# One PSUM ring of three double banks for scores, values and gate tiles, with score bursts of three chunks

## The chip, the cores and the metric

One core of a Trainium2 chip. The metric is the time of one execution in microseconds (us), measured on the device; all times below are us unless marked ns. Fast executions of one kernel spread over 1 to 5 us, so each comparison says how many runs it rests on. A time ratio is the mean over the fast runs of one kernel divided by the mean over the fast runs of the kernel before in the same rounds on the same chip, so it is not quite the ratio of the medians quoted. The comparisons were made on four occasions, each with its own runs of the kernel before; only ratios, and periods within one trace, are compared across them.

The granted clock (the share of full speed that TensorE got, averaged over an execution) differs between executions of one kernel and matters for such small differences. In executions at 0.993 to 0.996 the time is longer than in those at 0.998 or more: 375.3 (9 runs) against 373.5 (11) in e1, 376.1 (11) against 374.2 (8) in e3, 376.9 (7) against 375.1 (5) in e6. The two profiles in that state (e1, e6) show the clock halved for 3.4 us of the passage from batch 0 to batch 1, at 57.6 and 57.1, and not in the loop. Ratios of kernels with different shares of such executions have to be read with this in mind.

## The reference, cut to what matters

Causal attention over 8 batches and 8 heads, 576 queries of 64, with 16 extra "beacon" keys in front that every query sees, followed by a gated feed-forward layer on the 4608 tokens.

```python
scores = scale * np.matmul(q, k_all.transpose(0, 1, 3, 2))   # k_all: 16 beacons + 576 keys
scores = np.where(causal, -1e9, scores)
a = softmax(scores)                                          # written out in the reference
x = np.matmul(a, v_all)                                      # then to (4608, 512)
g = x @ w_gate                                               # 512 -> 1536
out = (gelu(g) * (x @ w_val)) @ w_out                        # 1536 -> 512
```

## The kernel before

The work is a loop over batches. In each, TensorE (PE) runs attention of batch b mixed with 48 output matmuls of batch b-1 (`o(n)` issues n of them), then 12 gate/value tiles. Heads go in four pairs. The causal scores of a pair are cut into four chunks, 0 to 3, of 512, 480, 464 and 208 columns; `scores(b, (m, c))` computes chunk c of pair m for both heads into one double PSUM bank, from which ScalarE takes the exponential. `av(b, m)` multiplies with the values into an `x_ps` tile and has VectorE normalize it into `y_sb`. GpSimd (POOL) zeroes the masked triangle of each diagonal tile, for b > 0, and also issues all casting loads, in order.

PSUM has eight banks: two double tiles for scores and gate tiles, one double tile for values, two single ones. The parts that matter (cuts marked `...`):

```python
psum_s = tile_pool("psum_s", bufs=2, PSUM)   # scores, gate/value: 2 x 2 banks
psum_t = tile_pool("psum_t", bufs=1, PSUM)   # 1 bank
psum_x = tile_pool("psum_x", bufs=1, PSUM)   # values: 2 banks
psum_o = tile_pool("psum_o", bufs=1, PSUM)   # 1 bank
...
warm(8, psum_x, "x")        # 8 matmuls of 512 columns, before the first data
...
if b:
    o(4);  scores(b, (0, 0)); scores(b, (0, 2))
    ...                            # batch 1 only: one transpose of its inputs
    ahead(2); o(7);  scores(b, (0, 1)); scores(b, (0, 3), (1, 3))
    ahead(2); o(7);  scores(b, (1, 0)); scores(b, (1, 2))
    av(b, 0); turn_dma(b, 0)
    o(4);  scores(b, (1, 1)); scores(b, (2, 0))
    ahead(2); o(7);  scores(b, (2, 1)); scores(b, (2, 2))
    av(b, 1); turn_dma(b, 1)
    o(4);  scores(b, (2, 3), (3, 3)); scores(b, (3, 0))
    o(6);  av(b, 2)
    scores(b, (3, 1)); scores(b, (3, 2))
    o(4);  turn(b, 2); put(b, 2)      # transposes of the result on PE
    o(5);  av(b, 3)
```

`ahead(n)` issues n loads for batch 2; it does something in batch 1 only, after an `ahead(5)` in front of the whole computation's masks. After the attention part come `load_v(b+1)`, `load_qk(b+2)` (GpSimd) and `transpose_dma(b+1)` (transposing loads from SBUF to SBUF on the sync queue).

The softmax here doesn't subtract the row's maximum and nothing guards it: scores larger than these inputs give would overflow.

## Time and profile before

| | before |
|---|---|
| time, median (4 runs of the first comparison) | 375.18 |
| profiled span | 372.9 |
| PE busy | 365.0 (98%) |
| period of the loop (starts of the same matmul in successive batches) | 39.72 |
| third gate tile of batch 0 starts at | 28.09 |
| first gate matmul on the single bank (`g_ps`), batch 1, starts at | 87.96 |

The last two rows cut the span into start, passage from batch 0 to batch 1, and loop; the whole argument uses these three pieces. The profile lines themselves stand in the prediction. One caution in reading them: ends of matmuls are modelled, and too late (a matmul of 512 columns is listed as 0.38 long where the next starts after 0.216), so idle time of PE is listed too short, and waits under 0.15 are not listed at all. Starts are to be trusted: the difference between two starts minus the known streaming time is what PE lost.

### The profile page before, as it was taken

Reading aid. Unit: us, or ns where it says so; the run is one execution under the profiler, and the core shown is the slowest. Engines: PE = TensorE matmul, PEld = TensorE weight load, DVE = VectorE, ACT = ScalarE, POOL = GpSimd, SP = SyncE. Lnnn points to the kernel's source line nnn. Section 1 sums busy time; section 2 is a strip of 40 time slices with the busy share of each in tenths; the row PEclk is TensorE's granted clock in tenths of the full one; section 3 lists DMA queues with packets and bytes.
Section 4 is the critical chain, followed back from the end, with each engine's and each line's share of the span. In section 5 each row is a group of like instructions: output and inputs, shape, how many; then the busy total and the mean of one; then the engine's idle time right before and its main releaser. Section 6 shows DMA issues by size and latency. Waiting matters only on the chain.

```text
span 372.9 us, 7489 instructions
## 1 busy us (share of the span) xinstructions
PE 365.0 (98%) x3030; PEld 181.7 (49%) x3030; DVE 151.7 (41%) x253; ACT 188.4 (51%) x240; POOL 166.1 (45%) x293
## 2 busy tenths in 40 slices
PE   7999989999999999999999999999999999999996
PEld 3664535544554446444554455445544464444443
DVE  3354643543344425433444335333444244424332
ACT  4864267435753487338733774357534873332210
POOL 8965578860478145843495148625600330000000
PEclk9699999999999999999999999999999999999999
DMA  7999999999169913999299929991590030000103
GB/s 102 123 177 197 205 161 145 135 145 114 46 123 143 154 37 94 152 134 90 62 142 152 88 78 126 125 142 48 120 161 16 33 87 30 0 0 30 56 33 109
DMA packets 152050, 38.33 MB, mean 103 GB/s; under 512 B 136528, under 2 KB 147536, under 8 KB 152016
## 3 DMA queue, kind: packets, MB, share of 16 engines
q0 software_dynamic: 107184, 19.13, 69.9%
q1 hardware_dynamic: 44832, 18.73, 27.2%
q8 instruction: 24, 0.39, 0.5%
q14 instruction: 10, 0.08, 0.1%
HBM read 38.27 MB, written 9.44 MB: 128 GB/s over the span
## 4 chain that ended last, share of the span: by engine, by line
PE 95%; DVE 2%; DMA 1%; ACT 1%; issue 1%; POOL 0%; POOLq 0%
PE gv_ps L173 46%; PE o_ps L173 26%; PE s_ps L173 8%; PE x_ps L173 8%; PE v_ps L173 2%; PE g_ps L173 1%; PE y_ps L181 1%; DMA qk<-in_k_dram 1%; PE t_ps L181 1%; DVE qkT L199 1%; DVE qkT L215 0%; DVE hT_sb L424 0%; ACT ge_sb L176 0%; ACT expT L176 0%; POOL qk L113 0%
## 5 line engine op out<-in xcount | busy, mean ns | idle before, releaser
L176 ACT ACTIVATE ge_sb<-gv_ps 128x512 bf16<-128x512 f32 x101 | 59.4, 597 | 133.0 <-PE gv_ps L173 133.0
L176 ACT ACTIVATE expT<-s_ps 128x960 bf16<-128x960 f32 (+3 forms) x112 | 101.8, 960 | 28.2 <-PE s_ps L173 24.9
L424 DVE TENSOR_TENSOR hT_sb<-gv_ps,ge_sb 128x512 bf16<-128x512 f32 x101 | 69.2, 691 | 106.2 <-ACT ge_sb L176 106.2
L173 PE MATMUL gv_ps<-xT_sb,wg_sb 128*128 128x512 bf16 x404 | 108.1, 379 | 0.0
L173 PE MATMUL gv_ps<-xT_sb,wv_sb 128*128 128x512 bf16 x404 | 108.1, 379 | 0.0
L173 PE MATMUL o_ps<-wo_sb,hT_sb 128*128 128x512 bf16 (+2 forms) x444 | 105.9, 374 | 0.0
L289 POOL TENSOR_SCALAR_AFFINE_SELECT expT<-expT 128x256 bf16<-128x256 bf16 (+2 forms) x140 | 51.7, 386 | 102.1 <-ACT expT L176 94.6
L173 PEld LDWEIGHTS <-wv_sb 128*128 128x128 bf16 x432 | 42.2, 98 | 51.8 <-DVE qkT L204 1.4
L173 PEld LDWEIGHTS <-wg_sb 128*128 128x128 bf16 x432 | 41.2, 98 | 46.7
L173 PEld LDWEIGHTS <-hT_sb 128*128 128x128 bf16 x444 | 38.7, 98 | 46.4 <-issue 8.9
L443 DVE COPY o_sb<-o_ps 128x512 f32<-128x512 f32 (+2 forms) x37 | 25.0, 676 | 44.0 <-PE o_ps L173 43.9
L113 POOL DMA_DIRECT2D v_sb<-in_v_dram x45 | 36.6, 837 | 3.0 <-DMA wo_sb<-in_moe_w_out_dram 1.7
L173 PE MATMUL s_ps<-qkT 64*128 64x512 bf16 (+5 forms) x384 | 36.2, 289 | 1.2 <-ACT qkT L176 0.7
L173 PEld LDWEIGHTS <-expT 128*128 128x128 bf16 (+1 forms) x960 | 32.3, 97 | 8.1 <-POOL expT L289 2.3
L113 POOL DMA_DIRECT2D k_sb<-in_k_dram x30 | 25.2, 844 | 21.7 <-DMA q_sb<-in_q_dram 13.2
L173 PE MATMUL x_ps<-v_sb,expT 128*128 128x65 bf16 x930 | 33.9, 193 | 0.6 <-issue 0.6
L113 POOL DMA_DIRECT2D q_sb<-in_q_dram x30 | 25.3, 887 | 3.6 <-DMA wo_sb<-in_moe_w_out_dram 3.6
L349 DVE TENSOR_TENSOR y_sb<-x_ps,r_sb 128x640 bf16<-128x640 f32 x31 | 25.6, 824 | 1.1
L173 PEld LDWEIGHTS <-qkT 64*128 64x128 bf16 x384 | 14.0, 95 | 21.6 <-issue 17.9
L347 DVE RECIPROCAL r_sb<-x_ps 128x10 f32<-128x10 f32 x31 | 6.9, 221 | 40.4 <-PE x_ps L173 40.4
L382 DVE COPY xT_sb<-y_ps 128x576 bf16<-128x576 bf16 x15 | 6.9, 458 | 11.5 <-PE y_ps L181 11.5
L610 ACT ACT_TABLE_LOAD x7 | 9.0, 1283 | 0.1
(50 smaller groups left out, 126.1 us busy)
## 6 DMA issues: line engine op xcount, KB each, us to landing
out_dram<-o_sb SPq DMA_DIRECT2D x35, 256.0 KB, 2.2
q_sb<-in_q_dram POOLq DMA_DIRECT2D x24, 128.0 KB, 9.1
v_sb<-in_v_dram POOLq DMA_DIRECT2D x21, 128.0 KB, 6.5
k_sb<-in_k_dram POOLq DMA_DIRECT2D x18, 128.0 KB, 9.9
wg_sb<-in_moe_w_gate_dram POOLq DMA_DIRECT2D x6, 256.0 KB, 8.9
wv_sb<-in_moe_w_val_dram POOLq DMA_DIRECT2D x6, 256.0 KB, 9.0
wo_sb<-in_moe_w_out_dram POOLq DMA_DIRECT2D x3, 512.0 KB, 11.9
v_sb<-in_v_dram POOLq DMA_DIRECT2D x7, 112.0 KB, 4.2
```

The source lines that it names most:

```text
L113: keep(nc.gpsimd.dma_start(out=out_ap, in_=in_ap))
L173: keep(nc.tensor.matmul(out_ap, lhsT, rhs, start=start, stop=stop, **kw))
L176: keep(nc.scalar.activation(out_ap, in_ap, func, **kw))
L181: keep(nc.tensor.transpose(out_ap, in_ap, ident[0:n, 0:n]))
L199: nc.vector.tensor_copy(qkT[:, m, :, NB:SK].rearrange("p w (t r) -> p w t r", r=6), t_ps[:, 0:2, 0:S].rearrange("p w (r t) -> p w t r", r=6),)
L289: nc.gpsimd.affine_select(out=d, in_=d, pattern=[[0, 2], [1, n]], compare_op=ALU.is_ge, fill=0.0, base=NB if t == 0 else 0, channel_multip ...
L347: keep(nc.vector.reciprocal(r, x[:, :, :, D:DV]))
L349: nc.vector.tensor_tensor(out=y_sb[:, :, h0:h1, :].rearrange("p j b d -> p b j d"), in0=x[:, :, :, 0:D], in1=r.to_broadcast([P, h1 - h0, 5 ...
L382: keep(nc.vector.tensor_copy(out_ap, y_ps[:, 0:S]))
L424: nc.vector.tensor_tensor(out=h_of[ci][:, fi, :], in0=gv_of.pop((ci, fi))[1], in1=ge_sb, op=ALU.mult)
L443: keep(nc.vector.tensor_copy(o_sb[:, ti, c0:c1], o_ps))
L610: keep(nc.scalar.preload_act_table_set(SET_GELU))
```

## The change

Its intent: give the double banks of the value tile to the ring, so that it has three, write score chunks in five bursts (four of three tiles, one of two) instead of seven of two, and let batch 0 run its chunks two ahead of ScalarE. The warm-up changes too: 100 matmuls of 64 columns.

```diff
-    psum_s = ... bufs=2
+    psum_s = ... bufs=3
-    psum_x = ...
...
-    warm(8, psum_x, "x")
+    warm(100)                       # 64 columns each, from the ring
-    transpose_half(0, 0, 1); transpose_half(0, 0, 0, by_act=True)
+    transpose_both(0, 0)
     c((0, 0)); c((0, 2))
...                                  # batch 0: transposes and chunks further apart
-            x = pool.tile(..., tag=where)          # psum_x by default
+            x = psum_s.tile([P, 2, 512], ..., tag="s")
...
             o(4)
             scores(b, (0, 0)); scores(b, (0, 2))
-            o(7)
             scores(b, (0, 1))
+            o(5); ahead(2); o(5)
             scores(b, (0, 3), (1, 3))
-            ahead(2); o(7)
             scores(b, (1, 0)); scores(b, (1, 2))
+            ahead(2); o(6)
             av(b, 0); turn_dma(b, 0)
-            o(4)
+            o(2)
             scores(b, (1, 1)); scores(b, (2, 0))
-            ahead(2); o(7); scores(b, (2, 1))
             scores(b, (2, 2))
+            ahead(2); o(6)
             av(b, 1); turn_dma(b, 1)
-            o(4)
+            o(2)
+            scores(b, (2, 1))
             scores(b, (2, 3), (3, 3)); scores(b, (3, 0))
-            o(6); av(b, 2)
+            o(10)
             scores(b, (3, 1)); scores(b, (3, 2))
-            o(4)
+            av(b, 2); o(5)
             turn(b, 2); put(b, 2)
-            o(5)
+            o(3)
             av(b, 3)
```

Transposes of batch 1 on PE move: two stay between gate tiles of batch 0, two now follow the first burst of batch 1.

More of the change, by code (lines that the diff above doesn't have):

```diff
@@ L73 @@
     opool = ctx.enter_context(tc.tile_pool(name="opool", bufs=2))
-    psum_s = ctx.enter_context(tc.tile_pool(name="psum_s", bufs=2, space=bass.MemoryType.PSUM))
+    psum_s = ctx.enter_context(tc.tile_pool(name="psum_s", bufs=3, space=bass.MemoryType.PSUM))
     psum_t = ctx.enter_context(tc.tile_pool(name="psum_t", bufs=1, space=bass.MemoryType.PSUM))
-    psum_x = ctx.enter_context(tc.tile_pool(name="psum_x", bufs=1, space=bass.MemoryType.PSUM))
     psum_o = ctx.enter_context(tc.tile_pool(name="psum_o", bufs=1, space=bass.MemoryType.PSUM))
@@ L81 @@
     ident = eye[:, 64:192]
-    idle = const.tile([P, 512], BF16, name="idle", tag="idle")
+    idle = const.tile([P, P], BF16, name="idle", tag="idle")
     nc.vector.memset(idle, 0.0)
@@ L194, in transpose_pe @@
     def transpose_pe(b, m):
-        t_ps = psum_x.tile([P, 2, 1024], BF16, name="t_ps", tag="x")
+        t_ps = psum_s.tile([P, 2, 1024], BF16, name="t_ps", tag="s")
         for w in range(2):
@@ L215, in transpose_half, with beacon_part, transpose_both, warm @@
             keep(nc.vector.tensor_copy(out_ap, in_ap))
-        if w:
-            keep(nc.vector.tensor_copy(qkT[:, m, 1, 0:NB], t_ps[:, S:SK]))
-    def warm(n, pool, tag):
-        w_ps = pool.tile([P, D_MODEL], FP32, name="w_ps", tag=tag)
+        return t_ps
+    def beacon_part(m, t_ps):
+        keep(nc.vector.tensor_copy(qkT[:, m, 1, 0:NB], t_ps[:, S:SK]))
+    def transpose_both(b, m):
+        k_ps = transpose_half(b, m, 1)
+        transpose_half(b, m, 0, by_act=m == 0)
+        beacon_part(m, k_ps)
+    def warm(n):
+        w_ps = psum_s.tile([P, 2, 512], FP32, name="w_ps", tag="s")
         for j in range(n):
-            mm(w_ps, idle[:, 128 * (j % 4) : 128 * (j % 4) + 128], idle, True, True)
+            mm(w_ps[:, 0, 0:D], idle, idle[:, 0:D], True, True)
     def transpose_dma(b):
@@ L300, with attend @@
     x_of = {}
-    def attend(b, m, where="x", heads=(0, 1)):
+    def attend(b, m, where="s", heads=(0, 1)):
         i = b * NPAIR + m
@@ L330, in attend_tiles @@
         else:
-            pool = psum_s if where == "s" else psum_x
-            x = pool.tile([P, 2, 512], FP32, name="x_ps", tag=where)
+            x = psum_s.tile([P, 2, 512], FP32, name="x_ps", tag="s")
             x_ps = (x[:, 0, :], x[:, 1, :])
@@ L386, with gv_mms @@
     gv_of = {}
-    def gv_mms(ci, fi, *kks, where="s", last=False):
+    def gv_mms(ci, fi, *kks, split=False, last=False):
         if (ci, fi) not in gv_of:
-            if where == "tx":
+            if split:
                 gv_of[ci, fi] = (
                     psum_t.tile([P, CH], FP32, name="g_ps", tag="t"),
-                    psum_x.tile([P, CH], FP32, name="v_ps", tag="x"),
+                    psum_s.tile([P, 2, CH], FP32, name="v_ps", tag="s")[:, 0, :],
                 )
             else:
-                pool = psum_s if where == "s" else psum_x
-                gv_ps = pool.tile([P, 2, CH], FP32, name="gv_ps", tag=where)
+                gv_ps = psum_s.tile([P, 2, CH], FP32, name="gv_ps", tag="s")
                 gv_of[ci, fi] = (gv_ps[:, 0, :], gv_ps[:, 1, :])
@@ L412, in gv_mms @@
         part(0)
-        if where != "tx":
+        if not split:
             part(1)
@@ L418, in gv_mms @@
         act(ge_sb, gv_of[ci, fi][0], ACT.Gelu)
-        if where == "tx":
+        if split:
             part(1)
@@ L427, in gv_mms, with gate_val @@
         )
-    def gate_val(ci, fi, where="s"):
-        gv_mms(ci, fi, *range(K_CHUNKS), where=where, last=True)
+    def gate_val(ci, fi, split=False):
+        gv_mms(ci, fi, *range(K_CHUNKS), split=split, last=True)
     def out_mm(ci, ti, fi, o_ps, c0=0, c1=D_MODEL):
@@ L509, with av @@
     ahead(5)
-    def av(b, m, where="x"):
+    def av(b, m, where="s"):
         attend(b, m, where)
@@ L518 @@
     keep(nc.scalar.preload_act_table_set(SET_EXP))
-    warm(8, psum_x, "x")
+    warm(100)
     keep(nc.vector.tensor_copy(qk6[0][1], kb_sb))
-    transpose_half(0, 0, 1)
-    transpose_half(0, 0, 0, by_act=True)
+    transpose_both(0, 0)
     c((0, 0))
     c((0, 2))
-    transpose_half(0, 1, 1)
-    transpose_half(0, 1, 0)
+    transpose_both(0, 1)
     c((0, 1))
     c((1, 0))
-    transpose_half(0, 2, 1)
     c((1, 2))
-    transpose_half(0, 2, 0)
+    transpose_both(0, 2)
     c((0, 3), (1, 3))
     c((1, 1))
-    transpose_half(0, 3, 1)
     c((2, 0))
-    transpose_half(0, 3, 0)
+    transpose_both(0, 3)
     c((2, 2))
     c((2, 1))
-    attend(0, 0, "x", (0,))
+    av(0, 0)
     c((3, 0))
-    attend(0, 0, "x", (1,))
-    normalize(0, 0)
     c((3, 2))
-    attend(0, 1, "ot", (0,))
+    av(0, 1, "ot")
     c((2, 3), (3, 3))
-    attend(0, 1, "ot", (1,))
-    normalize(0, 1)
     c((3, 1))
@@ L553 @@
     put(0, 1, by_act=True)
-    av(0, 3, "s")
+    av(0, 3)
     gv_mms(0, 0, 0)
@@ L558 @@
     keep(nc.scalar.preload_act_table_set(SET_GELU))
-    gv_mms(0, 1, 0, where="x")
+    gv_mms(0, 1, 0)
     turn(0, 3, psum_o, "o")
@@ L576 @@
             scores(b, (0, 2))
+            scores(b, (0, 1))
+            if b == 1:
+                transpose_pe(1, 2)
+            o(5)
+            ahead(2)
             if b == 1:
                 transpose_pe(1, 3)
-            ahead(2)
-            o(7)
-            scores(b, (0, 1))
+            o(5)
             scores(b, (0, 3), (1, 3))
-            ahead(2)
-            o(7)
             scores(b, (1, 0))
             scores(b, (1, 2))
+            ahead(2)
+            o(6)
             av(b, 0)
             turn_dma(b, 0)
-            o(4)
+            o(2)
             scores(b, (1, 1))
             scores(b, (2, 0))
+            scores(b, (2, 2))
             ahead(2)
-            o(7)
-            scores(b, (2, 1))
-            scores(b, (2, 2))
+            o(6)
             av(b, 1)
             turn_dma(b, 1)
-            o(4)
+            o(2)
+            scores(b, (2, 1))
             scores(b, (2, 3), (3, 3))
             scores(b, (3, 0))
-            o(6)
-            av(b, 2)
+            o(10)
             scores(b, (3, 1))
             scores(b, (3, 2))
-            o(4)
+            av(b, 2)
+            o(5)
             turn(b, 2)
             put(b, 2)
-            o(5)
+            o(3)
             av(b, 3)
@@ L619 @@
             if fi >= 2:
-                gate_val(b, fi, "x" if b and fi == 2 else "tx" if fi == F_TILES - 1 and b < B - 1 else "s")
-            if b == 0 and 8 <= fi < 11:
+                gate_val(b, fi, fi == F_TILES - 1 and b < B - 1)
+            if b == 0 and fi in (8, 9):
                 transpose_pe(1, fi - 8)
```

## The prediction

> **What bounds the kernel now.** I read the page first: busy shares, clock row, chain.
>
> ```profile
> PE 365.0 (98%) x3030; PEld 181.7 (49%) x3030; DVE 151.7 (41%) x253; ACT 188.4 (51%) x240; POOL 166.1 (45%) x293
> ...
> PEclk9699999999999999999999999999999999999999
> ...
> PE 95%; DVE 2%; DMA 1%; ACT 1%; issue 1%; POOL 0%; POOLq 0%
> ```
>
> TensorE (PE) is busy 98% of the span and makes 95% of the chain that ended last. Only the second slice has a low clock. Busy matmuls are modelled, so I read real rates from starts. In the windows view one period of the attention/feed-forward loop, and the attention part of it alone, look so:
>
> ```profile
> 88.83:128.55 39.72, 39.72 (x324) 19.47 (x322) 16.07 (x27) 22.34 (x28) 20.99 (x37) 1.00 1.19 113
> 89.69:108.43 18.74, 18.74 (x222) 9.81 (x221) 7.05 (x12) 15.23 (x16) 8.28 (x22) 1.00 0.46 76
> ```
>
> No PE idle in either. The waits view for PE lists only small items, all from the start and the passage from batch 0 to batch 1; these matter here:
>
> ```profile
> PE v_ps L173 <- DVE qkT L204: 0.9, 1, 0.9
> PE s_ps L173 <- ACT qkT L176: 0.7, 1, 0.7
> PE x_ps L173 <- issue: 0.6, 1, 0.6
> ```
>
> So there is little to win except what PE itself spends without streaming columns. The timeline of the second attention stage shows what happens round a score burst:
>
> ```profile
> 96.40 1.03 PE L173 MATMUL o_ps<-wo_sb,hT_sb 128*128 128x512 bf16 x4
> ...
> 96.60 0.22 DVE L347 RECIPROCAL r_sb<-x_ps 128x10 f32<-128x10 f32 x1 [2.14 <-PE x_ps L173]
> 96.85 0.82 DVE L349 TENSOR_TENSOR y_sb<-x_ps,r_sb 128x640 bf16<-128x640 f32 x1
> ...
> 97.36 0.60 PE L173 MATMUL s_ps<-qkT 64*128 64x64 bf16 x8
> ...
> 97.89 1.68 PE L173 MATMUL o_ps<-wo_sb,hT_sb 128*128 128x512 bf16 x7
> ```
>
> The reader should see two things. (1) Four output matmuls from 96.40 take 4 x 0.216 = 0.864 and would end at 97.26; the burst starts at 97.36. Entering costs 0.10. The burst has 480 + 512 columns, 0.42 of streaming, and takes 0.53: leaving costs 0.11. (2) The value tile (x_ps) whose matmuls end at 96.40 is read until 96.85 + 0.82 = 97.67, so its banks come free 1.27 us after PE went on. Pairs 1 and 2 give the same (101.01 to 102.28; 104.68 to 105.96).
>
> The start, by microsecond, in the windows view:
>
> ```profile
> 8.00:9.00 1.00, 0.83 (x19) 0.56 (x20) 0.92 (x3) 0.99 (x2) 1.00 (x2) 0.72 1.12 151
> ...
> 15.00:16.00 1.00, 1.00 (x24) 0.65 (x21) 0.76 (x3) 0.68 (x1) 1.00 (x3) 0.87 1.62 103
> ```
>
> The last columns but two are the granted clock: 0.72 in one, 0.87 in the other, 0.50 in between. If it switches between 1 and 0.5, it fell at 8.44 and rose at 15.26.
>
> **What the Trainium skill says.** "TensorE: Matmul & The Clock Gate", section "Back-to-back issue gap", gives N/2.4 + 2.5 ns at full clock: 215.7 ns for 512 columns. The trace agrees: 80 matmuls in 17.27 us are 215.9 each. This part is at its floor. The same page, "Part 1: The HAM clock gate", has the clock halved or released in free-running windows of 3413 ns. The trace agrees: 8.44 to 15.26 is 6.82, two windows, so an earlier edge lies at 5.03. "TensorEngine Tiling (Array Packing)", section "Key Properties", says that a change of tiling mode drains TensorE. Scores use 64 rows, the output, value and gate matmuls 128; the 0.10 and 0.11 agree with that. "PSUM — Partial Sum Buffer", section "PSUM bank collisions raise a hardware error", asks for semaphores by bank: a score may not enter a bank before its last reader is through. In the trace PE starts about 0.05 after such a release (values ready at 25.18, weights loaded from them at 25.23).
>
> **The change part by part, per batch of the loop.**
>
> *Five bursts for seven.* One period is 39.72. From it come 144 gate, value and output matmuls of 512 columns at 0.216 (31.09), four value stages (95.47 to 96.40, 0.93 each: 3.72) and two transposes of the result (106.17 to 106.43, 0.26 each: 0.52). 4.39 are left for scores. Four pairs of 512 + 480 + 464 + 208 = 1664 columns, both heads beside each other, at 0.216/512 stream 2.81. Of the 1.58 above that, 0.14 is waiting: the second tiles of [chunk 1; chunk 3] and of pair 2's [chunk 1; chunk 2] each want a ring buffer some 0.07 before its exponential is done (99.70 against 98.78 + 0.95 + 0.05). 1.44 over seven bursts is 0.21 each, as read above. Two bursts less save 0.42, the deeper ring the 0.14: **-0.56**.
>
> *The value tiles move into the ring.* The allocations of one batch run: scores 00, 02, 01, 03, 10, 12, **value 0**, 11, 20, **22**, **value 1**, 21, 23, **30**, 31, 32, value 2, value 3. With three buffers each tile needs the one three places earlier. Score 22 then waits for value 0 to be normalized, score 30 for value 1. Between the end of the value stage and score 22 PE has only two output matmuls (0.43), the entry (0.10) and chunks 11 and 20 (0.42): 0.95. The banks are free after 1.27 + 0.05 = 1.32. Wait: 0.37. For score 30 the work is 0.43 + 0.10 + 0.38 (480 + 416 columns) = 0.91; wait: 0.41. Before, value tiles had banks of their own.
>
> *Transpose of pair 2.* Between value stage 2 and its transposes there were two chunks of scores and four matmuls; now there are five matmuls, 1.08, and the normalized values come after about 1.33. Wait: 0.25.
>
> *The exponentials as feeders.* A burst of three makes 2.8 us of ScalarE work. I set the exponentials end to end from the measured starts and durations: burst 1 at 90.65, first exponential 0.49 later, third done at 93.9; the third tile of burst 2 wants that buffer at 90.65 + 0.72 + 2.16 + 0.10 + 0.39 = 94.02. It just fits, and later bursts have more room; GpSimd's masks are done before each value stage too. No new wait.
>
> Sum: -0.56 + 0.37 + 0.41 + 0.25 = **+0.47 per batch**, so +2.8 for batches 2 to 7.
>
> *Batch 0 to batch 1.* The listed 0.95 at v_ps and about 0.2 at t_ps go away, for transposes alternate with gate tiles in a ring of three. One transpose moves out of batch 0's feed-forward into batch 1, cost unchanged. But in batch 1 the first one follows the burst and wants score 00's buffer 0.72 after that burst's start, free only after 0.49 + 0.95 + 0.05: about 0.75 of wait, and some 0.2 more at score 12. With the +0.47 this is **about +0.3**; I call it 0 to 0.5.
>
> *The start.* Eight warm-up matmuls of 512 columns were 0.427 apart (weight loads 2.23, 2.66, 3.08) and ended at 4.8, just before the first keys (4.92). A hundred of 64 columns at that slow rate are 53 ns each: about 70 until the edge at 5.03, the other 30 at 31 ns (a value stage has 30 in 0.93), end near 6.0. The first transposes start 1.05 later. For this, ScalarE should be better fed: 14 exponentials at 5.43/6 = 0.905 are 12.7 us, but they lie between 7.13 and 21.88, so 2.05 are gaps. With chunks two ahead perhaps 1.5 of them close, if the clock stays up. But the window after the warm-up again has transposes waiting for copies, and the clock can fall one window later. I count the start as **-0.5 to +1.0, mean +0.3**; the 0.6 marked issue may or may not stay.
>
> Total: 2.8 + 0.3 + 0.3 = +3.4, shaded to +2.5 since each wait rests on an order of buffers that I infer: **378.0 us**.
>
> **Rivals.**
> 1. *The waits do not come*, because the ring hands out buffers otherwise than strictly in turn, or normalization is quicker. For it: the intent is evidently a ring of three that never blocks. Against: the order follows from the program, and 1.27 is measured three times. Then it is 7 x -0.56 = -3.9, the passage -1, the start 0: about 370.5, still within 2%.
> 2. *The start decides.* The clock stays up after the longer warm-up, gaps close, the stall of 0.6 goes: -2.5 on top of the loop's waits, some 376. Against: the first window after the warm-up is little denser than the one that throttled.
> 3. *ScalarE becomes the bound.* It is busy 15.23 of 18.74 in the attention stage, and the fit at score 12 has 0.1 of room. If each of three bursts waits 0.3 more, add 6 us: 384. Against: average load 81%, and ten output matmuls lie ahead of two of the bursts.
>
> **Range and chances.** My chain gives 376 to 380 with the start's spread, and the three runs before differ by 2 us. 80% range: **374.5 to 380.5**. Faster by over 2% (below 368) needs more than all waits gone: **0.03**. Slower by over 2% (above 383) needs rival 3: **0.04**. Within 2%: **0.93**.
>
> **What would show it.** In the profile after: a period of 40.2 instead of 39.72; PE waits listed as s_ps for DVE y_sb (or its instruction), about 0.4, twice per batch, and y_ps for y_sb, about 0.25, once; entry gaps five times; no wait of v_ps for qkT; one t_ps wait for ACT expT of about 0.7 in batch 1; first transposes near 6.0. If the period is 39.2 without these waits, the step on the ring's order is wrong. If s_ps waits for ACT expT in most bursts, the step on the exponentials is.

## The result, and the profile after

The changed kernel takes 378.89 (median of 4, 378.57 to 380.98) against 375.18: ratio 1.0102, interval 1.0054 to 1.0151. A second measurement, on another occasion, gave 1.0102 again (1.0067 to 1.0137). It is slower by 1%, inside the range and within 2%.

The page after:

```profile
PE 363.0 (96%) x3122; PEld 183.3 (49%) x3122; DVE 151.3 (40%) x253; ACT 186.5 (50%) x240; POOL 166.1 (44%) x293
...
PEclk9999999999999999999999999999999999999999
...
PE 78%; DMA 8%; DVE 6%; POOL 6%; issue 1%; POOLq 0%
```

The windows view of one period, and PE's waits (who waited, total, times, longest):

```profile
89.54:129.76 40.22, 39.67 (x323) 19.41 (x322) 16.07 (x27) 22.13 (x28) 21.01 (x37) 1.00 1.21 107
```

```profile
PE s_ps L172 <- DVE y_sb L354: 3.2, 14, 0.2
PE x_ps L172 <- POOL expT L295: 1.6, 1, 1.6
...
PE t_ps L180 <- ACT expT L175: 0.7, 1, 0.7
PE o_ps L172 <- DMA wo_sb<-in_moe_w_out_dram: 0.7, 1, 0.7
```

PE now falls idle within the period, 14 times (twice in each of seven batches) for `y_sb`, the normalized values. The low clock of the second slice is gone. The chain that ended last, 95% PE before, now has GpSimd, VectorE and DMA in it. Where the 3.7 of span (372.9 to 376.6) come from:

| piece | before | after | difference | predicted |
|---|---|---|---|---|
| up to the third gate tile of batch 0 | 28.09 | 25.81 | -2.28 | +0.3 |
| from there to `g_ps` of batch 1 | 59.87 | 62.70 | +2.83 | +0.3 |
| five periods (`g_ps` of batch 1 to 6) | 198.60 | 201.27 | +2.67 | +2.35 |
| the rest (attention of batch 7, last tiles) | 86.3 | 86.9 | +0.5 | +0.47 |

So the loop did as predicted. The start gained what it was not expected to gain, and the passage lost it again. The experiments ask about each.

The timeline of PE in the loop after:

```profile
97.11 0.59 PE L172 MATMUL o_ps<-wo_sb,hT_sb 128*128 128x512 bf16 x2
97.63 0.60 PE L172 MATMUL s_ps<-qkT 64*128 64x64 bf16 x8
98.44 0.37 PE L172 MATMUL s_ps<-qkT 64*128 64x464 bf16 x2 [0.21 <-DVE y_sb L354]
...
101.49 0.56 PE L172 MATMUL s_ps<-qkT 64*128 64x64 bf16 x10
102.29 0.39 PE L172 MATMUL s_ps<-qkT 64*128 64x512 bf16 x2 [0.24 <-DVE y_sb L354]
...
106.31 1.24 PE L172 MATMUL o_ps<-wo_sb,hT_sb 128*128 128x512 bf16 x5
107.65 0.43 PE L180 MATMUL y_ps<-eye,y_sb 112*128 112x112 bf16 x5
```

Work it out from starts. The burst at 97.63 has streamed its first two chunks by 97.63 + 0.42 = 98.05; score 22 starts at 98.44, 0.39 late (the list says 0.21, since ends are modelled late). Score 30 could start at 101.49 + 0.38 = 101.87 and starts at 102.29: 0.42. The transposes could start at 106.31 + 5 x 0.216 = 107.39 and start at 107.65: 0.26, a wait that the list does not even show. Predicted were 0.37, 0.41 and 0.25.

### The profile page after: what moved, and what is told of

Same layout as the page of the kernel before. It is cut to its first block, busy times and chain, and to the rows that moved or that the text cites. A ratio compares the mean times of both kernels' runs of the same rounds, so it can differ in the third digit from the quotient of the medians.

```text
span 376.6 us, 7661 instructions
## 1 busy us (share of the span) xinstructions
PE 363.0 (96%) x3122; PEld 183.3 (49%) x3122; DVE 151.3 (40%) x253; ACT 186.5 (50%) x240; POOL 166.1 (44%) x293
## 4 chain that ended last, share of the span: by engine, by line
PE 78%; DMA 8%; DVE 6%; POOL 6%; issue 1%; POOLq 0%
PE gv_ps L172 41%; PE o_ps L172 21%; PE x_ps L172 7%; DVE y_sb L354 5%; PE s_ps L172 5%; DMA wo_sb<-in_moe_w_out_dram 3%; DMA qk<-in_q_dram 3%; POOL v_sb L112 2%; DMA wv_sb<-in_moe_w_val_dram 2%; PE v_ps L172 1%; PE g_ps L172 1%; DVE r_sb L352 1%; PE y_ps L180 1%; POOL qk L112 1%; POOL q_sb L112 1%
## 5 line engine op out<-in xcount | busy, mean ns | idle before, releaser
L175 ACT ACTIVATE expT<-s_ps 128x960 bf16<-128x960 f32 (+3 forms) x112 | 99.8, 965 | 28.6 <-PE s_ps L172 28.0
L172 PE MATMUL s_ps<-qkT 64*128 64x512 bf16 (+5 forms) x384 | 33.8, 281 | 5.3 <-DVE y_sb L354 3.2
## 6 DMA issues: line engine op xcount, KB each, us to landing
wo_sb<-in_moe_w_out_dram POOLq DMA_DIRECT2D x3, 512.0 KB, 11.9
```

The source lines that it names most:

```text
L172: keep(nc.tensor.matmul(out_ap, lhsT, rhs, start=start, stop=stop, **kw))
L175: keep(nc.scalar.activation(out_ap, in_ap, func, **kw))
```

## The experiments

Ten runs, all with correct results. `e` numbers are edits of the changed kernel unless said otherwise. Periods are differences between starts of the first `g_ps` matmul in successive batches, so they are exact to some 0.02 in one profile.

### The loop: three waits, seven or five bursts

**e1_space.** The output matmuls are spread so that the value tile is free before the score that needs its banks.

```diff
-            o(6); av(b, 0); turn_dma(b, 0); o(2)
+            o(4); av(b, 0); turn_dma(b, 0); o(4)
-            o(6); av(b, 1); turn_dma(b, 1); o(2)
+            o(4); av(b, 1); turn_dma(b, 1); o(4)
-            o(5); turn(b, 2); put(b, 2); o(3)
+            o(7); turn(b, 2); put(b, 2); o(1)
```

> The changed kernel with the same 48 output matmuls per batch spread otherwise: four instead of two after value stages 0 and 1 (two fewer before each), and seven instead of five between value stage 2 and its transposes (one instead of three after). Theory (the ring's order makes score 22, score 30 and the transposes wait 0.37, 0.42 and 0.26 per batch): all three waits vanish, the period of the loop falls from 40.23 to 39.16, about 0.56 under the 39.72 of the kernel before; time near 378.9 - 7 x 1.05 = 371.5. Rival A (bursts of three are fed too slowly by ScalarE, the waits only move to the exponentials): the period stays above 39.9 and waits for ACT expT appear. Rival B (fewer bursts save nothing, the switch between 64 and 128 rows is free): the period is 39.6.

Measured: median 374.14 (20 runs), ratio 0.9937 (0.9916 to 0.9958); the expected time of 371.5 was missed (373.5 in the executions at a clock of 0.998 or more). All waits for `y_sb` are gone from PE's list; in three of five periods it is 39.31, in the other two 39.95 and 39.78. The timeline of one such batch shows where the 0.15 above 39.16 are:

```profile
97.39 1.08 PE L172 MATMUL x_ps<-v_sb,expT 128*128 128x65 bf16 x30
...
100.87 1.23 PE L172 MATMUL x_ps<-v_sb,expT 128*128 128x65 bf16 x30
101.93 1.03 PE L172 MATMUL o_ps<-wo_sb,hT_sb 128*128 128x512 bf16 x3
```

The first value stage has its usual 1.08; the second has 1.23, and PE goes on 1.06 after its start instead of 0.93. Two output matmuls fewer stand in front of it, so it may now wait 0.13 for its masks; e8 tests that. (The same view shows 3 output matmuls where there are 4: some records are missing in this trace, and the "issue" waits of 0.16 in its list are these holes.) The two long periods wait for something else, the transposing loads of the next batch, taken up below.

**e2_value.** Only the first two of these three changes.

> Only the first half of that: four output matmuls after value stages 0 and 1; the transposes of pair 2 left as in the changed kernel. Theory: the two waits of s_ps for DVE y_sb go, the one before y_ps of about 0.26 stays; period 40.23 - 0.79 = 39.44. If the three waits are one queue (one hides another), the period would be clearly different from 39.44, by more than 0.1.

Measured: four of five periods 39.57 or 39.58 (the fifth, 40.34, waits for transposing loads), single time 374.8. That is 39.44 + 0.13, the same extra wait of value stage 1 as in e1; e2 minus e1 is 0.27, the wait of the transposes. The waits are separate and add.

**e3_seven.** The ring of three with the bursts of the kernel before.

```diff
             scores(b, (0, 0)); scores(b, (0, 2))
-            scores(b, (0, 1))
             if b == 1: transpose_pe(1, 2)
-            o(5); ahead(2)
+            ahead(2); o(7); scores(b, (0, 1)); scores(b, (0, 3), (1, 3)); ahead(2)
             if b == 1: transpose_pe(1, 3)
-            o(5); scores(b, (0, 3), (1, 3))
-            scores(b, (1, 0)); scores(b, (1, 2)); ahead(2); o(6)
+            o(7); scores(b, (1, 0)); scores(b, (1, 2))
             av(b, 0); turn_dma(b, 0)
-            o(2)
+            o(4)
...                                  # and so on, as in the kernel before
```

> The changed kernel's ring of three, start and batch 0, but seven bursts of two chunks in the order of the kernel before. Theory: no tile three places after a value tile is wanted early, so no wait for y_sb; against the kernel before only the two waits of 0.07 for exponentials go; period 39.58, that is 0.42 above e1 (two bursts at 0.21). Time near 375. Rival (value tiles in the ring cost by themselves, whatever the order): waits for y_sb remain and the period is 39.9 or more. Rival (burst count is free): e3 equals e1.

Measured: ratio 0.9976 (0.9958 to 0.9995, 20 runs); all five periods 39.59 or 39.60, no wait for `y_sb`. So the shared ring is harmless as such, and a period is 0.13 shorter. What costs is the order: a value tile three places ahead of a score that comes soon after it.

### The start: what gained, and why it came to nothing

**e5_oldwarm.** The changed kernel with the old warm-up. **e6_newwarm.** The kernel before with the new one.

```diff
# e5, in the changed kernel
-    mm(w_ps[:, 0, 0:D], idle, idle[:, 0:D], True, True)          # warm(100), D = 64
+    mm(w_ps[:, 0, :], idle[:, 128 * (j % 4) : 128 * (j % 4) + 128], idle, True, True)   # warm(8)
# e6, in the kernel before
-    mm(w_ps, idle[:, 128 * (j % 4) : 128 * (j % 4) + 128], idle, True, True)            # warm(8)
+    mm(w_ps[:, 0:D], idle[:, 0:P], idle[:, 0:D], True, True)     # warm(100)
```

> The changed kernel with the old warm-up (8 matmuls of 512 columns) in place of 100 of 64. It tells the two parts of the start apart. Theory A (the gain of 2.3 at the third gate tile, 25.8 against 28.1, comes mostly from the clock, which did not fall after the longer warm-up): the first transposes are at 4.9, the clock falls near 8.4 in most executions, and the third gate tile starts at 27 or later. Theory B (it comes from chunks two ahead keeping ScalarE fed): the third gate tile starts at 26.0 or earlier although the clock falls. By either, the whole time stays within 0.5 of the changed kernel, since what batch 0 wins is given back at batch 1's masks.

> The kernel before with only the new warm-up (100 matmuls of 64 columns, weights of 128). Theory A: no low clock in the second slice, third gate tile near 26.5. Theory B: it stays near 28 even at full clock. By either the whole time is within 0.3% of the kernel before, because batch 1's masks wait behind load issues that stand at fixed clock times; its executions with granted clock 0.991 are already no slower (375.6) than those with 1.0 (376.4).

The changed kernel ran once more in the same rounds as a control:

> The changed kernel once more, unaltered, as the control for the runs of this call. Expected: about 1.010 of the kernel before, as in its first four runs; if it lies nearer 1.006, the gain of e4_ahead (1.0036) is smaller than it looked.

Measured:

| | first transposes | clock low from, to | third gate tile | ratio |
|---|---|---|---|---|
| before | 4.92 | 8.44, 15.26 | 28.09 | 1 |
| e6_newwarm | 6.33 | not in the start | 26.74 | 0.9993 (0.9971 to 1.0014) |
| e5_oldwarm | 4.67 | 7.76, 14.58 | 26.94 | 1.0101 (1.0065 to 1.0137) |
| after, first and second profile | 5.67, 5.75 | never | 25.81, 26.25 | 1.0102, 1.0102 |

The low clock is worked out from the windows view as in the prediction; e5's rows that give its edges are

```profile
7.00:8.00 1.00, 0.98 (x20) 0.71 (x21) 0.00 (x0) 0.48 (x1) 1.00 (x3) 0.88 1.14 158
...
14.00:15.00 1.00, 1.00 (x26) 0.61 (x20) 0.00 (x0) 1.00 (x2) 1.00 (x2) 0.71 1.48 94
```

and they lie 6.82 apart again, two of the windows that the Trainium skill gives in "TensorE: Matmul & The Clock Gate". Theory A is borne out in the main. The new warm-up alone brings 1.35 although its first transposes are 1.4 later. Counted from the first transposes to the third gate tile, the kernel before takes 23.17 with the clock low and 20.41 without (e6); the changed kernel's order takes 22.27 with it low (e5) and, in the nine profiles that have both order and warm-up (also e1 to e4 and e7 to e9), 19.92 to 20.50 without. So the clock is worth 2 to 3 and the order at most 1, about 0.3 at full clock, where one profile (e6) stands against nine. The third gate tile of these nine starts at 25.69 to 26.89, since the warm-up's length varies by about 1 between executions.

In the means none of it is seen at the end: e6 over the kernel before is 0.9993, and e5 (1.0101) is not told from the changed kernel (1.0102), each known to some 0.2 to 0.4%. The 54 fast runs of the kernel before beside e1 to e4 say something similar: mean 375.57 in the 14 with granted clock 0.992 or less (the profile in this state has the low clock at the start), 376.38 in the 19 with 0.998 or more, 376.97 in the 21 between. The five executions of e6 at 0.998 or more, mean 375.06, hint at a gain that the seven others hide; that is not settled.

**Where it goes.** GpSimd in the passage, before and after:

```profile
47.05 0.88 POOL L113 DMA_DIRECT2D q_sb<-in_q_dram  x1 [1.81 <-DMA wo_sb<-in_moe_w_out_dram]
49.70 3.31 POOL L113 DMA_DIRECT2D q_sb<-in_q_dram  x4 [1.77 <-DMA wo_sb<-in_moe_w_out_dram]
52.99 0.78 POOL L289 TENSOR_SCALAR_AFFINE_SELECT expT<-expT 128x224 bf16<-128x224 bf16 x2
```

```profile
47.36 0.88 POOL L112 DMA_DIRECT2D q_sb<-in_q_dram  x1 [1.81 <-DMA wo_sb<-in_moe_w_out_dram]
49.95 3.31 POOL L112 DMA_DIRECT2D q_sb<-in_q_dram  x4 [1.71 <-DMA wo_sb<-in_moe_w_out_dram]
53.23 1.41 POOL L295 TENSOR_SCALAR_AFFINE_SELECT expT<-expT 128x224 bf16<-128x224 bf16 x4
```

PE's first scores of batch 1 come at 50.32 before and at 45.73 after (part of it because one more transpose now follows them), but the first mask comes at 53.0 and 53.2: it stands behind five load issues, and these stand until earlier loads have landed. In all eight profiles with these loads in front the first mask starts at 52.9 to 53.9, whether the first scores come at 45.7 or at 50.3. The Trainium skill ("TensorE: Matmul & The Clock Gate", table of specifications) lists GpSimd's queue as strictly first in, first out; this trace agrees.

**e4_ahead.** The loads leave the way.

```diff
-    ahead(5)                           # in front of all masks
...
             scores(b, (0, 1)); ... o(5)
-            ahead(2)
+            ahead(3)
...
             scores(b, (1, 2))
-            ahead(2)
+            ahead(3)
...
             scores(b, (2, 2))
-            ahead(2)
+            ahead(3)
...
             scores(b, (3, 0))
+            ahead(2)
             o(10)
```

> The changed kernel with the first five loads of batch 2's queries no longer queued on GpSimd ahead of batch 1's masks, but spread after the bursts of batch 1 (3, 3, 3, 2). Theory: GpSimd works in order, and its load issues stand still until earlier transfers land, at the same clock time in both kernels; so the 2.3 us won at the start are lost again at the masks (x_ps waits 1.6 for POOL expT). Without those issues in front this wait goes, the wait of 0.7 for the output weights stays, since their landing is set by the transfers; time 1.3 to 1.8 below the changed kernel, about 377.3; the period unchanged at 40.23. Rival (the transfers as such, not the queue's order, hold batch 1): another wait of the same size takes its place, and the time stays within 0.5 of the changed kernel.

Measured: ratio 1.0036 (1.0022 to 1.005, 20 runs) against 1.0102, so 0.66% or 2.5 better (known to some 0.4%), more than expected. Part of that is the clock: three of the changed kernel's eight executions were under 0.998, one of these 20. In all, with the loads out of the masks' way (e4, e7 to e9) it is one of 32; in e1, e3 and e6, with loads in front, 28 of 52. Whether PE's wait for the masks brings the low clock is not tested. The first mask of batch 1:

```profile
47.56 0.37 POOL L295 TENSOR_SCALAR_AFFINE_SELECT expT<-expT 128x224 bf16<-128x224 bf16 x1 [2.29 <-ACT expT L175]
...
49.88 2.64 POOL L112 DMA_DIRECT2D q_sb<-in_q_dram  x3
```

It now waits for the exponential alone. From the third gate tile to `g_ps` of batch 1 it takes 86.23 - 26.11 = 60.12, against 62.70 and, before, 59.87. The wait for the masks is gone. The wait for the output weights is no longer listed, but single starts show that it stays in part, as expected: the fifth output matmul after the transpose starts at 49.43 where 48.94 + 0.22 = 49.16 was possible, 0.27 late, and the weights landed at 49.39. In the changed kernel it starts at 49.70 instead of 48.85, 0.85 late. PE came 0.31 later to it in e4, and the weights 0.27 earlier; what made them earlier is not separated. The period stayed 40.23 (one of five 40.38).

### Putting it together

**e7_both** is e1 and e4 in one kernel.

> e1_space and e4_ahead together: output matmuls spread round the value stages, and the first loads of batch 2 no longer in front of batch 1's masks. If the two losses are separate they add: e1 took 1.010 to 0.994 (16 thousandths), e4 took 1.010 to 1.0036 (6); together about 0.988, some 371.7. Rival: with a period of 39.2 the transposed loads for the next batch (waits of s_ps for DMA qkT, 0.5 in two of six periods of e1) become the bound and take the second gain back: 0.991 or more.

Measured: median 372.52 (4 runs), ratio 0.9895 (0.9865 to 0.9925), halfway between the two expectations. Four periods are 39.31 or 39.32, one is 40.68, waiting for transposing loads.

**e8_mask**: one output matmul moved in front of value stage 1.

```diff
-            o(4); av(b, 1)
+            o(5); av(b, 1)
...
-            o(10); scores(b, (3, 1))
+            o(9);  scores(b, (3, 1))
```

> e7_both with five output matmuls instead of four ahead of value stage 1 (nine instead of ten ahead of the last burst). In e1 and e7 the period is 39.31, not the 39.16 worked out; value stage 1 takes 1.06 there against 0.93, the two masks of chunk 11 end some 0.13 late. Theory: the stage falls to 0.93 and the period to 39.18; over six batches 0.8, time some 0.2% under e7. Rival (the 0.15 is not the mask): period stays at 39.31.

Measured: median 371.52, ratio 0.9843 (0.9792 to 0.9894; 4 runs, all at clock 0.998 or more). The three undisturbed periods are 39.16. So value stage 1 did wait for masks, and the sum in the prediction, without its waits, is met: 39.72 - 0.56 = 39.16. But two of five periods are now 40.42 and 40.26. PE's waits:

```profile
PE s_ps L172 <- DMA qkT<-k_sb: 1.6, 2, 1.1
```

The next batch's keys, transposed by DMA, are not there in time. Single waits show which keys, in e8 and, with seven bursts, in e3:

```profile
167.39 0.76 PE L172 MATMUL s_ps<-qkT 64*128 64x512 bf16 x8
169.23 0.21 PE L172 MATMUL s_ps<-qkT 64*128 64x80 bf16 x2 [1.08 <-DMA qkT<-k_sb]
```

```profile
170.43 0.58 PE L172 MATMUL s_ps<-qkT 64*128 64x512 bf16 x4
172.56 0.56 PE L172 MATMUL s_ps<-qkT 64*128 64x64 bf16 x10
```

The last piece of chunk 1, 80 columns wide, needs the keys that are transposed last. A first burst of three wants it 0.59 after its first matmul; in the order with seven bursts chunk 1 opens the second burst, and the piece is wanted 2.32 after. By the trace these keys land between 1.2 before and 1.9 after that first matmul, and late ones occur in both orders: in e3 once 1.58 after (172.00), and nothing waited. So in the three profiles with seven bursts none of 15 periods is lengthened, and in the nine with five bursts 14 of 45 are, by 0.1 to 1.4 (in the changed kernel's first profile one, by 0.15; in its control one, 41.13 for 40.23). Merging the bursts took 1.7 of slack from the transposing loads, a cost that neither the prediction nor the expectations had. It takes back much of the saving: e1 is only 0.7 to 0.8 under e3 at equal clock, where 39.31 for 39.59 over seven batches would be 2.0; in e1's profile the two long periods add 1.1.

**e9_later**: `load_qk(b + 2)` three gate tiles later, behind the transposing loads.

```diff
             if fi == 0:
                 ...
-                if b and b + 2 < B:
-                    load_qk(b + 2)
                 if 2 <= b + 1 < B:
                     transpose_dma(b + 1)
+            if fi == 3 and b and b + 2 < B:
+                load_qk(b + 2)
```

> e8_mask with the loads of the batch after next issued three gate tiles later, behind the transposed loads of the next batch rather than beside them. In e7 one period of six was 40.68 instead of 39.31, with scores waiting for transposed keys that landed 8.5 after issue. Theory (these share the transfer engines with the loads): the transposed loads land sooner, all six periods are 39.2, and the time is 0.2 to 0.5% under e8. Rival (the loads then end in the attention stage and hold GpSimd's masks): periods of 40 and more, with waits for POOL expT in the loop.

Measured: ratio 0.9863 (0.9817 to 0.991), no better than e8 (the intervals overlap). The two long periods shrink to 39.87 and 39.73 but do not go, and the time from issue to landing of the transposing loads (median 7.7 in e8, 7.6 in e9) hardly changes. The theory is not borne out; why the transposes of some batches land later than those of others stays open.

## Why the prediction was right or wrong

**The time** was right: 378.89 for 378.0. The loop, which makes most of the difference, was right by its mechanism. That start and passage came out near their predicted sum is luck: two terms were wrong and cancel, which the prediction did not foresee. (Its sum before shading, 3.4 over the median of 375.5 that it had, is 378.9.)

- *Five bursts for seven save 0.42.* Right. With no waits in either, seven bursts have a period of 39.59 (e3) and five 39.16 (e8, undisturbed periods): 0.43. That the bursts of three want the last keys 1.7 earlier was left out; in the changed kernel's first profile it cost 0.15 in one period of five.
- *The deeper ring saves 0.14.* Right: 39.72 to 39.59 (e3).
- *Values in the ring: 0.37 and 0.41; transposes 0.25.* Right: 0.39, 0.42, 0.26, and taking them away gives 39.31 in e1, where 0.13 of a new wait are left.
- *The exponentials just feed a burst of three.* Right: no burst in the loop waits for them.
- *Batch 0 to 1, "about +0.3".* The step that failed is that only PSUM order was looked at here. Where GpSimd's masks do not stand behind loads, the passage costs 60.12 - 59.87 = 0.25 (e4), near the 0.3 worked out, the wait of 0.71 for score 00's exponential included and 0.27 for output weights besides. But the trace of the kernel before already showed GpSimd standing until 53.0; a PE that comes sooner could not get its masks sooner. Masks (1.6 in the list of waits) and output weights (0.85 by starts, 0.27 in e4) make most of the 2.6 more that the changed kernel lost.
- *The start, "-0.5 to +1.0".* Wrong in sign: -2.28. The term mis-sized is the clock: "the clock can fall one window later" was reckoned as a risk, and the gain of its not falling left to rival 2. It did not fall there in any of the ten profiles with the new warm-up, and that is worth 2 to 3 counted from the first transposes (e5, e6); the 1.5 of closing gaps are 0.3 to 0.9. What in the longer warm-up keeps the clock up is not shown. The warm-up ended at 5.67, not 6.0, since the edge to full clock came at 4.42 and not at 5.03 in that execution (starts 53 to 54 ns apart until 4.40, 29 to 30 after); in others it ended as late as 6.65.
- *Rival 1* (no waits) and *rival 3* (ScalarE bound) are refuted by the lists of waits; *rival 2* was right about the clock at the start and, for the kernel as changed, wrong that its gain reaches the end.

What the change teaches is in the control: the same ring and bursts, with output matmuls placed so that the value tile is free in time and loads not in front of masks, have a mean 1.6% under the kernel before (e8, interval 1.1 to 2.1%), where the change as made is 1.0% above it. Part of the 1.6% is the clock: e8's four executions are at 0.998 or more, five of the seven beside them are not; against the other two (375.9) e8's mean of 371.4 is 1.2% lower. In the profiles (372.9 and 370.3) the start gives 2.4 of the difference, five periods of the loop only 0.45, the end 0.5, and the passage takes 0.8: with masks out of the way the gain of the start does reach the end, and late keys eat most of what the bursts save.

## What to carry to other kernels

When tiles of different lifetimes share a ring, write down the order of allocations and, for each tile, the one that is as many places ahead as the ring is deep; a tile that is read late (here 1.27 after its last matmul) must not be that one for work that comes soon after. Fill the gap with independent work of that length. Before counting a gain at the start, look for queues that stand at fixed times, such as loads in front of compute on one in-order engine: a stage that comes sooner only waits longer there. And before merging bursts, look at what else their order gave time to: here the keys that land last.

## What the Trainium skill lacked or had wrong

- "TensorEngine Tiling (Array Packing)", section "Key Properties", says that a change of tiling mode drains TensorE but gives no size. Here it is 0.10 in and 0.11 out for 128 to 64 rows and back, and 0.43 for two pairs of changes by e3 against e8.
- "TensorE: Matmul & The Clock Gate" speaks of idle and busy windows and gives no share of activity between them. Here PE was busy 0.37 to 0.89 in each full microsecond (5 to 8, transposes and half-height scores) of the window before the clock fell in the kernel before; in the changed kernel 1.00, 0.41 and 0.84 from 8 to 11 (its window runs from 7.83 to 11.25, by the trace's record of the clock) brought no fall. The same page's "Back-to-back issue gap", used in the prediction, gives N/2.4 + 2.5 ns for a single matmul and some 131 ns per 512 columns for a stream; here a stream of 80 ran at 215.9, the figure for the single one.
- "DMA: Bandwidth & Descriptors", section on the anatomy of a DMA from GpSimd, fits 2.0 + bytes/436e3; an estimate from it for 512 KB is 3.2. Here such a load took a median of 11.9 beside others, and, which the page does not say, GpSimd stood 1.7 to 1.8 before further issues until earlier loads had landed.
